# Sixteen stores of output rows asked for by GpSimd instead of SyncE

## The chip, the cores and the metric

The kernel runs on one core of one Trainium2 chip. A core has five engines that run beside each other: TensorE (PE; its weight loads are listed as PEld), VectorE (DVE), ScalarE (ACT), GpSimd (POOL) and SyncE (SP). Each works off its own queue in order. Transfers between the memories are asked for ("issued") by an engine's queue and carried out by 16 DMA engines that all queues share; a semaphore tells when a transfer has landed. The metric is the device time in microseconds (us); smaller is better.

## The reference, cut to what matters

A state-space convolution and a linear attention over the same length are mixed by a gate:

```python
x = A_u                                              # 1 x 2048 x 512
g = sigmoid((x * gate_w).sum(-1, keepdims=True))
# A: K = Re(sum_n C * exp(dt*A*l) * dt*B), y = irfft(rfft(u) * rfft(K))[:L] + u * Dskip
a = A_ref(x, A_re, A_im, B_re, B_im, C_re, C_im, log_dt, Dskip)
# B: 32 heads of 16: phi = [softmax(q w), softmax(-q w)]; o = phi_q (phi_k^T v) / (phi_q . sum phi_k); o @ wo
b = B_ref(B_x, wqkv, w_phi, wo)
return g * a + (1 - g) * b
```

The kernel writes one output, `out`, 2048 rows of 512 bf16 values, 2 MB.

## The kernel before, in words

All steps are nodes of one plan (`class Plan`). A node names an engine, a function that emits its instructions, and the nodes it depends on. The order in which the nodes are emitted is written out as a string of two-digit numbers (`ORDER`, line 74) and replayed by `Plan.run` (line 149); on each engine the instructions run in that order, each as soon as its semaphores allow. For nodes that can stand on either of two engines, a second string (`SIDES`) says which; `P.cur.at` is the engine of the node at hand. A transfer (`P.dma`, line 128) is a node on SP, or on SP or ACT where `eng=("SP", "ACT")` is given. Between queues nothing but semaphores orders the work.

The 512 channels are four quarters Q = 0 to 3 of 128. For each quarter the convolution kernel is generated in units of 32 channels (`kgen`, lines 1098 to 1120), brought to the frequency domain, multiplied with the input's spectrum that waits in DRAM (`XUX`), and brought back (`transform`, line 1190). For a "far" transform the half-done result `Zr` is written to DRAM (`Zd`, lines 1277 and 1279) and read back in another order (`ZT`, line 1289); both are issued by SP. The last product of a transform goes to PSUM (`psy`, line 1345 for a far one, line 1358 for the other kind), and VectorE multiplies it with the gate into the tile `xT` (lines 1367, 1370 and 1373), which by then holds the output. The last quarter is done in three transforms: units 12 and 13 together (64 channels, far), unit 14 (32 channels, far), and unit 15 (32 channels, not far).

The attention runs in four blocks of 512 rows (`block`). The first three add to the same PSUM tiles as the convolution. The last, block 3, is late: its result `bps` is brought to `xT` by ScalarE and VectorE (line 980 among others) for three quarters of the columns, all at once.

`xT` holds row 64 q + 4 j + c of the output in partition 32 c + q, at index j. A store therefore takes one c (32 partitions), a range of j, and a range of columns. There are two places that store, each of them a function `st(h)` that issues two stores, for c = 2h and 2h + 1:

- line 992, from node `outL` (line 995): the rows of block 3 (four j), 384 columns; four stores of 96 KB.
- line 1384, from node `out` (line 1398): after the transform of Q = 1 the columns of quarters 0 and 1 (12 j, 256 columns, four stores of 192 KB); after Q = 2 its 128 columns (12 j, four of 96 KB); after units 12 and 13 their 64 columns (16 j, four of 64 KB); and after unit 15 the last 64 columns (16 j, four of 64 KB). This last set is the one with `last` true. `SIDES` puts one of its two nodes on ACT; all other nodes of both places are on SP.

In `ORDER` the stores stand in this order: Q = 2, then Q = 0 and 1, then half of units 12 and 13, half of block 3, the other halves of both, and the last set. SP's queue has the write of the last `Zd` after the first four stores and the read of the last `ZT` after the next four.

GpSimd does the index ramps, masks and some fills at the start; it issues no transfer.

Of the kernel before, what the change touches and what calls it, by code (L numbers as in the profile page):

```python
# [10 lines left out]
ACT = mybir.ActivationFunctionType  # L11
# [798 lines left out]
def plan_queries(P, nc, g, psum, r):  # L810

    fc, act, at, xT = g.fc, g.act, g.at, g.xT
# [12 lines left out]
    def block(b, late, yn=()):  # L825
        Q, L = Bag(), "L" if late else ""
        eq = []
        a = None
        nm = 2 if late else 1
        for m0 in range(0, 4, nm):  # L830
# [19 lines left out]
            a = P.add("PE", "pq" + L, pq, [sh, sp] + g.Wqn + r["xt"] + ([a] if a else []), take=([psq] if late else ["bk"]) + ([] if m0 else ["r8"]))  # L850
# [64 lines left out]
        pb, po, ot, out = None, None, [], []  # L915
# [47 lines left out]
        for ip in range(2 if late else 0):  # L963
            j = 4 * b + 2 * ip
# [24 lines left out]
        if late:  # L989
            def st(h):  # L990
                for c in (2 * h, 2 * h + 1):
                    (nc.scalar if P.cur.at == "ACT" else nc.sync).dma_start(out=g.out2d[:, 0:384].rearrange("(q j c) d -> c q j d", q=32, j=16, c=4)[c][:, 4 * b:4 * b + 4],
                                      in_=xT[32 * c:32 * c + 32, 4 * b:4 * b + 4, 0:3, :].rearrange("p j a d -> p j (a d)"))
            for h in range(2):
                P.dma("outL", 1.2, 2.0, lambda h=h: st(h), on, move=0.8, cnt=2, eng=("SP", "ACT"))
# [61 lines left out]
def plan_conv(P, nc, g, psum, r):  # L1057

    fc, act, at, xT = g.fc, g.act, g.at, g.xT
# [130 lines left out]
    def transform(XA, ready, Q, off, nd, far, Ls, last, co=0, free=True, split=False):  # L1190
# [5 lines left out]
        pair = 1 if Q == 1 else 0  # L1196
        lo = 64 if last else off
        ov = g.out2d[:, 128 * (Q - pair) + lo:128 * Q + off + nd].rearrange("(q j c) d -> c q j d", q=32, j=16, c=4)
# [5 lines left out]
        for r0 in range(0, 32, ns):  # L1204
# [24 lines left out]
            def tt(k=None, r0=r0, box=box, end=end):  # L1229
# [11 lines left out]
                if k != 0:  # L1241
# [3 lines left out]
                    if not far:  # L1245
                        F.tt = box.t.rearrange("p k (r d) -> p k r d", d=nd)
                        box.t = None
            b = P.add("PE", "psB%d" % nd, sb, ready + [sk] + ([b] if r0 else []), take=[psq, "XK"] + (["r8"] if first else []),
                      drop=(["XA0"] if end and XA.drop else []))
# [68 lines left out]
        for j0 in range(0, 16, nj):  # L1318
# [62 lines left out]

            def st(h, js=slice(0, 12 if Q < 3 else 16)):
                for c in (2 * h, 2 * h + 1):
                    (nc.scalar if P.cur.at == "ACT" else nc.sync).dma_start(out=ov[c][:, js], in_=xT[32 * c:32 * c + 32, js, Q - pair:Q + 1, lo:off + nd].rearrange("p j a d -> p j (a d)"))
            ya = []
            if Q < 3:
                ya = [P.add("PE", "pya", pya, [sq] + [n for b in range(j0 // 4, min(3, j0 // 4 + 2)) for n in g.ot[b]] + ([y] if j0 else []), take=[psq], rw=("diagD", ""))]
# [8 lines left out]
            if end and Q != 0 and (nd > 32 or last):  # L1396
                for h in range(2):
                    P.dma("out", 1.2, 2.0, lambda h=h, st=st: st(h), on, move=(1.6 if pair else 1.05 if far and nd == 128 else 0.9), cnt=2, eng=("SP", "ACT"))
                on.clear()
# [18 lines left out]
    for k, (units, far) in enumerate(g.LAST):  # L1418
# [6 lines left out]
        off = 32 * (units[0] - 12)  # L1425
# [205 lines left out]
```

## Time and profile before

| | before |
|---|---|
| median of three runs | 260.86 us (260.01 to 261.76) |
| profiled execution, its own time | 259.96 us |
| its span, first to last instruction | 258.2 us |
| PE, DVE, ACT, POOL busy | 197.2, 227.3, 224.4, 11.2 us |
| stores of the output | 20: 18 issued by SP, 2 by ACT |

The profile's page gives busy times, a strip of 40 slices of 6.5 us, the chain of work that ended last and the costliest groups. A row of the timeline has the start in us from the start of the span, the length in us, the engine (a "q" behind it: its queue, that is, an issue), the line of the code, the operation, what it writes and reads, and how many instructions are merged. The listing of transfers gives the size of each and the median time from issue to landing. A row of the waits has who waited, for whom, the sum in us, how often, and the longest. A row of the windows has a stretch of time and how long each engine was busy in it.

### The profile page before, as it was taken

What the parts mean: (1) busy time and instruction counts of PE and PEld (TensorE: products, weight loads), DVE (VectorE), ACT (ScalarE), POOL (GpSimd) and SP (SyncE); (2) the same over time, 40 slices, a digit from 0 to 9 for tenths busy, and PEclk for the clock granted to TensorE, in tenths of its full rate; (3) what the DMA queues carried; (4) which work ended last, traced back from release to release, by engine and by line L of the source; (5) the groups of instructions that cost most, each with busy time, mean ns of one, the idle gap of its engine ahead of it and who ended that gap; (6) DMA issues with size and microseconds to landing.
All of it is one profiled execution on the core that took longest, in us unless ns stands there. A gap on an engine that the chain in (4) does not pass through costs nothing.

```text
span 258.2 us, 10095 instructions
## 1 busy us (share of the span) xinstructions
PE 197.2 (76%) x4512; PEld 132.2 (51%) x4512; DVE 227.3 (88%) x308; ACT 224.4 (87%) x312; POOL 11.2 (4%) x21
## 2 busy tenths in 40 slices
PE   0577899999962888789576858688977679989750
PEld 0466665665642542356345535474764556765530
DVE  6888799797899998999999999999999999978710
ACT  6999979998999999999999999999997989756210
POOL 5650000000000000000000000000000000000000
PEclk9999999999996587999979998999999999999985
DMA  6899100083710669105451449525768789776875
GB/s 200 142 206 208 45 3 1 5 250 70 226 30 0 201 198 280 63 4 161 130 135 34 120 110 244 164 46 162 193 157 212 196 217 252 208 219 120 200 101 98
DMA packets 67259, 36.19 MB, mean 140 GB/s; under 512 B 46352, under 2 KB 62864, under 8 KB 66832
## 3 DMA queue, kind: packets, MB, share of 16 engines
q1 hardware_dynamic: 66160, 35.42, 55.0%
q8 instruction: 35, 0.57, 0.9%
q10 hardware_dynamic: 1056, 0.13, 0.3%
q14 instruction: 8, 0.07, 0.1%
HBM read 22.17 MB, written 13.37 MB: 138 GB/s over the span
## 4 chain that ended last, share of the span: by engine, by line
ACT 43%; PE 35%; issue 7%; SPq 7%; DVE 4%; DMA 2%; ACTq 0%
ACT cs L68 9%; PE pk L705 6%; ACT Eq L68 5%; PE vp L753 4%; SPq L1497 4%; ACT XA L145 4%; ACT E L68 4%; PE psz L1263 3%; ACT L65 3%; ACT XK L145 3%; ACT Zr L145 3%; ACT xst L145 3%; PE psy L820 3%; PE kps L179 2%; ACT trg L68 2%
## 5 line engine op out<-in xcount | busy, mean ns | idle before, releaser
L1098 DVE TENSOR_TENSOR A<-Ctab,Dtab 128x2048 bf16<-128x2048 bf16 x32 | 38.7, 1222 | 0.8 <-PE kps L179 0.8
L68 ACT ACTIVATE cs<-args 128x1024 bf16<-128x1024 f32 x32 | 31.2, 1068 | 0.0
L179 PE MATMUL kps<-R,A 128*32 128x64 bf16 x1536 | 17.3, 199 | 7.9 <-DVE R L1120 1.9
L179 PEld LDWEIGHTS <-A 128*32 128x32 bf16 x1536 | 15.4, 116 | 11.9 <-DVE R L1120 4.0
L1120 DVE TENSOR_TENSOR R<-E,cs 128x2048 bf16<-128x2048 bf16 x16 | 19.5, 1222 | 0.0
L1116 DVE TENSOR_TENSOR R<-E,cs 128x2048 bf16<-128x2048 bf16 x16 | 19.4, 1222 | 0.0
L1263 PE MATMUL psz<-t,TI 128*128 128x512 bf16 x60 | 15.7, 387 | 3.4 <-ACT cs L68 1.5
L145 ACT CAST XK<-psB 128x1024 bf16<-128x1024 f32 (+1 forms) x17 | 16.8, 1016 | 0.4 <-PE psB L192 0.4
L145 ACT CAST Zr<-psz 128x1024 bf16<-128x1024 f32 x15 | 15.5, 1036 | 1.8 <-PE psz L1263 1.1
L1231 DVE TENSOR_TENSOR t<-XUX,XK 128x2048 bf16<-128x2048 bf16 x14 | 17.1, 1222 | 0.0
L68 ACT ACTIVATE E<-args 128x1024 bf16<-128x1024 f32 x16 | 17.1, 1066 | 0.0
L753 PE MATMUL vp<-WW,xT 128*128 128x512 bf16 x64 | 17.0, 398 | 0.0
L839 PE MATMUL pq<-xT,Wqp 128*128 128x512 bf16 x64 | 16.7, 405 | 0.3 <-ACT E L68 0.3
L68 ACT ACTIVATE Ek<-pk 128x512 bf16<-128x512 f32 x32 | 16.7, 600 | 0.2
L68 ACT ACTIVATE Eq<-pq 128x512 bf16<-128x512 f32 (+1 forms) x28 | 16.8, 695 | 0.2 <-PE pq L839 0.2
L612 PE MATMUL psB<-XAu,TB 64*128 64x128 bf16 x256 | 11.7, 256 | 6.2 <-ACT XAu L145 4.1
L145 ACT CAST XA<-psA 128x1024 bf16<-128x1024 f32 x15 | 15.1, 1046 | 0.2 <-PE psA L186 0.2
L705 PE MATMUL pk<-WW,xT 128*128 128x512 bf16 x64 | 15.2, 380 | 0.0
L612 PEld LDWEIGHTS <-TB 64*128 64x128 bf16 x256 | 10.0, 114 | 9.5 <-issue 9.0
L762 DVE TENSOR_TENSOR vr<-vb,vr 128x1024 bf16<-128x1024 bf16 x16 | 10.6, 688 | 3.0 <-ACT vr L68 2.7
L147 DVE CAST XAu<-psA 128x1024 bf16<-128x1024 f32 x9 | 10.6, 1218 | 2.7 <-PE psA L587 2.7
L65 ACT ACT_TABLE_LOAD x10 | 12.8, 1283 | 0.2
(206 smaller groups left out, 495.0 us busy)
## 6 DMA issues: line engine op xcount, KB each, us to landing
XUX<-XUd SPq DMA_DIRECT2D x32, 256.0 KB, 4.2
XUd<-xst SPq DMA_DIRECT2D x8, 512.0 KB, 3.3
ax<-apd SPq DMA_DIRECT2D x16, 256.0 KB, 4.8
Zd<-Zr SPq DMA_DIRECT2D x15, 256.0 KB, 4.1
ZT<-Zd SPq DMA_DIRECT2D x12, 256.0 KB, 4.8
UD<-in_A_u_dram SPq DMA_DIRECT2D x16, 128.0 KB, 4.4
XUd<-xst SPq DMA_DIRECT2D x8, 256.0 KB, 4.0
wqk<-in_B_wqkv_dram SPq DMA_DIRECT2D x1, 1024.0 KB, 5.7
```

What stands on the lines that cost most here:

```text
L65: return self.nc.scalar.preload_act_table_set(name)
L68: return self.nc.scalar.activation(**kw)
L145: self.nc.scalar.copy(out=o, in_=i)
L179: nc.tensor.matmul(kps[32 * dj:32 * dj + 32, g4, e, :], lhsT=A[:, d // 4, 32 * ka:32 * ka + 32, d % 4], rhs=R[:, kr, d, :], start=(i == 0) ...
L612: nc.tensor.matmul(box.ps[:, c2, sl, :], lhsT=fc.TB[rows, b0:b0 + 2].rearrange("p a b -> p (a b)"), rhs=X.t[rows, k, r0 + sl].rearrange("p ...
L705: nc.tensor.matmul(box.ps[:], lhsT=xT[:, st, kt, :], rhs=g.WW[:, kt, :], start=(kt == 0), stop=(kt == 3))
L753: nc.tensor.matmul(box.ps[:], lhsT=xT[:, st, kt, :], rhs=g.WW[:, 4 + kt, :], start=(kt == 0), stop=(kt == 3))
L1098: nc.vector.tensor_tensor(out=c.A[:, :, 64 * k:64 * k + 64, :].rearrange("p q (x b) l -> p x b q l", b=8), in0=cf.unsqueeze(2).to_broadcas ...
L1116: nc.vector.tensor_tensor(out=c.R[:, :, :, 32:64], in0=t.E[:, 1].unsqueeze(1).to_broadcast([128, 2, 32, 32]), in1=t.cs[:], op=ALU.mult)
L1120: nc.vector.tensor_tensor(out=c.R[:, :, :, 0:32], in0=t.E[:, 0].unsqueeze(1).to_broadcast([128, 2, 32, 32]), in1=t.cs[:, ::-1, :, ::-1], o ...
L1231: nc.vector.tensor_tensor(out=box.t, in0=Ls[r0 // ns].X[:], in1=box.XK[:].unsqueeze(1).to_broadcast([128, 2, 1024]), op=ALU.mult)
L1263: nc.tensor.matmul(box.ps[:, hb, :], lhsT=fc.TIp[:, k].rearrange("p h a t -> p (h a t)"), rhs=box.t[:, k, 512 * hb:512 * hb + 512], start= ...
```

## The change

At both places the issuing engine becomes GpSimd. At line 1384 the last set is left out of this: it stays on ACT for one half and on SP for the other. So 16 of 20 stores move: four of 192 KB, eight of 96 KB and four of 64 KB. What is stored, from where and to where is unchanged, and so are `ORDER` and `SIDES`: the nodes are emitted at the same places, only onto another queue.

```diff
         if late:
             def st(h):
                 for c in (2 * h, 2 * h + 1):
-                    (nc.scalar if P.cur.at == "ACT" else nc.sync).dma_start(out=g.out2d[:, 0:384].rearrange("(q j c) d -> c q j d", q=32, j=16, c=4)[c][:, 4 * b:4 * b + 4],
+                    nc.gpsimd.dma_start(out=g.out2d[:, 0:384].rearrange("(q j c) d -> c q j d", q=32, j=16, c=4)[c][:, 4 * b:4 * b + 4],
                                       in_=xT[32 * c:32 * c + 32, 4 * b:4 * b + 4, 0:3, :].rearrange("p j a d -> p j (a d)"))
...
             def st(h, js=slice(0, 12 if Q < 3 else 16)):
                 for c in (2 * h, 2 * h + 1):
-                    (nc.scalar if P.cur.at == "ACT" else nc.sync).dma_start(out=ov[c][:, js], in_=xT[32 * c:32 * c + 32, js, Q - pair:Q + 1, lo:off + nd].rearrange("p j a d -> p j (a d)"))
+                    (nc.scalar if P.cur.at == "ACT" else nc.sync if last else nc.gpsimd).dma_start(out=ov[c][:, js], in_=xT[32 * c:32 * c + 32, js, Q - pair:Q + 1, lo:off + nd].rearrange("p j a d -> p j (a d)"))
```

## Prediction, written before the result was known

> **What bounds the kernel now.** I read the page first, then the chain of waits, then the last 21 us queue by queue, because nothing is stored to the output before that.
>
> ```profile
> span 258.2 us, 10095 instructions
> ...
> POOL 5650000000000000000000000000000000000000
> ```
>
> The last GpSimd work ends near 16 us; its queue is empty afterwards. The listing of DMA issues gives the stores:
>
> ```profile
> out_dram<-xT SPq DMA_DIRECT2D x8, 96.0 KB, 2.8
> out_dram<-xT SPq DMA_DIRECT2D x4, 192.0 KB, 4.7
> ...
> out_dram<-xT SPq DMA_DIRECT2D x6, 64.0 KB, 2.3
> ...
> out_dram<-xT ACTq DMA_DIRECT2D x2, 64.0 KB, 2.8
> ```
>
> That is 20 stores: 18 on SP, two on ACT. The last set is four of 64 KB, two on SP and two on ACT; the other 16 move. In order of time (start, length, engine, line), SP's queue and then what the stores wait for:
>
> ```profile
> 236.95 3.00 SPq L1384 DMA_DIRECT2D out_dram<-xT  x4
> 240.06 0.43 SPq L1279 DMA_DIRECT2D Zd<-Zr  x1
> 240.53 3.18 SPq L1384 DMA_DIRECT2D out_dram<-xT  x4
> 243.83 3.54 SPq L1289 DMA_DIRECT2D ZT<-Zd  x4
> 247.48 2.20 SPq L1384 DMA_DIRECT2D out_dram<-xT  x2
> 249.78 1.05 SPq L992 DMA_DIRECT2D out_dram<-xT  x2
> 250.87 2.12 SPq L1384 DMA_DIRECT2D out_dram<-xT  x2
> 253.04 1.29 SPq L992 DMA_DIRECT2D out_dram<-xT  x2
> 254.43 1.27 SPq L1384 DMA_DIRECT2D out_dram<-xT  x2
> ```
>
> ```profile
> 235.71 1.22 DVE L1370 TENSOR_TENSOR xT<-psy,gT 128x1024 bf16<-128x1024 f32 x1
> ...
> 242.52 1.22 DVE L1370 TENSOR_TENSOR xT<-psy,gT 128x1024 bf16<-128x1024 f32 x1
> 243.66 1.13 DVE L980 TENSOR_SCALAR xT<-bps,gT 128x384 bf16<-128x384 f32 x2
> ...
> 251.44 0.69 DVE L1370 TENSOR_TENSOR xT<-psy,gT 128x512 bf16<-128x512 f32 x1 [0.74 <-PE psy L1345]
> ```
>
> ```profile
> 237.11 1.01 ACT L145 CAST Zr<-psz 128x1024 bf16<-128x1024 f32 x1
> ...
> 252.21 1.37 ACTq L1384 DMA_DIRECT2D out_dram<-xT  x2
> ```
>
> SP is backed up. The last arithmetic ends at 251.44 + 0.69 = 252.13. ACT asks for its half of the last set at once, at 252.21. SP's half has the same data but stands behind eight other stores and goes out at 254.43, 2.3 us later. The windows around these issues give issue-to-landing times, first for ACT's second store, then for the pair of 96 KB, then for SP's last pair:
>
> ```profile
> out_dram<-xT ACTq DMA_DIRECT2D x1, 64.0 KB, 3.1
> ```
>
> ```profile
> out_dram<-xT SPq DMA_DIRECT2D x2, 96.0 KB, 2.6
> ```
>
> ```profile
> out_dram<-xT SPq DMA_DIRECT2D x2, 64.0 KB, 2.2
> ```
>
> SP's last store starts half way through the pair, at 254.43 + 0.64 = 255.07, and lands at 255.07 + 2.2 = 257.27. The closing steps take 258.2 - 257.27 = 0.93. So SP's queue sets the end, not an engine. The profiled execution took 259.96 us, 1.76 more than its span, and 0.9 below the median of the runs, 260.86; I apply the sum to both.
>
> **What leaves SP.** 16 issues: 3.00 + 3.18 + 2.20 + 1.05 + 2.12 + 1.29 = 12.8 us of SP's queue. Two things stood behind them. First, SP's half of the last set: it can go at 252.2, and its second store at 252.2 + 0.64 = 252.8. ACT's second store starts at about 252.21 + 0.69 = 252.9 and lands 3.1 later, at 256.0. The other landing row, 2.2, would make it 255.1; I take 3.1, because GpSimd's stores will be in flight beside it. Second, the small round trip over DRAM of the last far set: Zr is done at 237.11 + 1.01 = 238.12, but its write goes out only at 240.06, behind four stores, 1.9 us late, and the read back ZT stands behind four more. With SP free, ZT lands about 2 us sooner. What that is worth is read from who waits for it:
>
> ```profile
> PEld L1345 <- DMA ZT<-Zd: 0.4, 1, 0.4
> ...
> PE psz L1301 <- issue: 1.3, 1, 1.3
> PE psy L1358 <- issue: 1.2, 1, 1.2
> ```
>
> TensorE waited 0.4 us for ZT before the last product; ahead of it, it is held by the other product L1358 and by gaps that no releaser explains ("issue", 1.3 and 1.2 us), which I leave as they are. So 0.4 us of the 2 us comes out: the last arithmetic ends at 251.7. SP's and ACT's end becomes 256.0 - 0.4 = 255.6, and with 0.93 the span 256.5.
>
> **What is added.** GpSimd gets 16 issues in a row. They keep their order, so the four whose data are ready at 235.71 + 1.22 = 236.93 come first, and the four of 192 KB, which SP asks for at 240.53 without a wait for data, stand behind them. The rest is ready at 242.52 + 1.22 = 243.74 and 243.66 + 1.13 = 244.79, before GpSimd gets there if an issue takes over (243.74 - 236.93) / 8 = 0.85 us. Nothing else is queued behind these waits on GpSimd, and no engine waits for a store; only the end does. With p us for one issue, the last one is out at 236.93 + 16p and lands 2.6 later (the 96 KB row, the size of the last one); this reaches 255.6 at p = 1.0, today's 257.27 at p = 1.11, and 2.6 us more, one per cent of the time, at p = 1.27. Each 0.1 us of p is 1.6 us of time. This price decides the case, and the trace has no DMA issued by GpSimd. The nearest rows, from SP's issues of the same stores and from GpSimd's own instructions:
>
> ```profile
> L1384 SPq DMA_DIRECT2D out_dram<-xT x14: 321/602/1594, 237.0 to 255.1; - x14
> ```
>
> ```profile
> 10.41 2.34 POOL L454 TENSOR_TENSOR selE<-m,b 128x1024 bf16<-128x1024 bf16 x1
> ...
> 13.85 0.86 POOL L487 MEMSET SSw<- 128x264 bf16 x1
> ...
> 15.25 0.12 POOL L491 MEMSET eps<- 128x1 f32 x1
> ```
>
> From below: 0.32, SP's shortest, which hides everything behind the readiness of the data; GpSimd's own instruction overhead, 0.12, is lower still. From above: 2.34, its dearest instruction, which ends at 236.93 + 37.4 + 2.6 + 0.93 = 277.9. I take 1.0: above SP's median 0.60 and just above the 0.86 of a GpSimd instruction that writes a few hundred elements, since a store is not one run of bytes: by its access pattern it is 32 partitions by 4, 12 or 16 rows, thus 128, 384 or 512 pieces, and somebody has to list them. The last store then lands at 236.93 + 16.0 + 2.6 = 255.5, level with the last set's 255.6.
>
> The Trainium skill speaks against the change here: "DMA: Bandwidth & Descriptors", section "SWDGE vs HWDGE vs iDMA", says that DMAs from GpSimd have their descriptors written by a program on its cores, and "Latency and other measured facts" gives about 1 us to the first byte, against 0.6 from SP. No run so far shows it; by that extra 0.4 us GpSimd's last store would land at 255.9 and the gain would be 1.4 instead of 1.7 us.
>
> The sum: 258.2 - 256.5 = 1.7 us off. Own time 259.96 - 1.7 = 258.3; against the median 260.86 - 1.7 = 259.2. A measurement of this kernel (runs from 260.01 to 261.76) can tell about one per cent, 2.6 us, from no change, so this counts as within it.
>
> **Rivals.**
>
> *GpSimd becomes the bound (slower).* Its place is the row of 16 issues from 236.93, its price p, and it decides from p = 1.11. For it: GpSimd is slow per element (0.86 us for 264 elements of a memset), and 12 of the 16 stores have 384 or 512 pieces. Against: SP needs 0.60. At p = 1.5 the last store lands at 236.93 + 24 + 2.6 = 263.5, the span is 264.5, and the time 260.86 + 6.3 = 267.1.
>
> *VectorE locks GpSimd out (slower).* If GpSimd cannot list pieces while VectorE works, VectorE's busy time is added to its row:
>
> ```profile
> core 0: us, PE busy (x) PEld busy (x) DVE busy (x) ACT busy (x) POOL busy (x), PEclk, DMA share, GB/s
> 236.90:245.00 8.10, 6.86 (x250) 4.96 (x249) 5.84 (x10) 2.66 (x5) 0.00 (x0) 1.00 0.78 171
> 245.00:252.10 7.10, 3.28 (x203) 2.36 (x203) 1.51 (x3) 1.07 (x2) 0.00 (x0) 0.82 0.75 106
> ...
> 236.90:258.20 21.30, 10.15 (x453) 7.32 (x452) 7.39 (x13) 3.73 (x7) 0.00 (x0) 0.80 0.71 129
> ```
>
> VectorE (DVE) is busy for 7.39 us. GpSimd ends at 236.93 + 16 + 7.4 = 260.3, the last store lands at 262.9, span 263.9: 260.86 + 5.7 = 266.5. Against it: most of VectorE's operations there read psy, psA or bps at full f32 size and not two bf16 tiles. The rule stands in the Trainium skill, "SBUF — State Buffer", in the box on the "DVE blocks DMA" trap, which names VectorE's two-port modes, and says elsewhere that tensor_tensor has none; no run here has shown it.
>
> *The transfers bound the end (no effect).* In the last of these rows the 16 DMA engines are busy 0.71 of the time (the share ahead of the GB/s). If GpSimd's stores are still queued on them when the last set goes out, its landing stretches, as the 192 KB stores' 4.7 does; then 252.9 + 4.7 + 0.93 = 258.5, and the time is 260.86 + 0.3 = 261.2. About the same time results where p lies a little over 1.11.
>
> *More comes out.* If the last set lands in 2.2 instead of 3.1 and GpSimd is done by then, the span is 256.5 - 0.9 = 255.6; a gap of 1.2 on TensorE that shrinks with quieter queues would add to that. The time is 259.2 - 0.9 = 258.3, or down to 257.1 with such a gap gone.
>
> That the stores would stay on SP is excluded by the diff: lines 992 and 1384 name the engine.
>
> **How the numbers follow.** Forecast 0.42, at 259.2, its own range 258.3 (the last set lands in 2.2) to 260.7 (p = 1.1). GpSimd as the bound by over one per cent 0.28; VectorE's lock 0.04; no effect 0.16; more comes out 0.10. Faster by over one per cent: the last case and a little of the forecast, 0.13. Slower by over one per cent: the first two, 0.32. The rest, 0.55, within. The range is 257.6 to 267.1: below, the middle of the case in which more comes out; above, p = 1.5, with about 0.1 left out at either end.
>
> **What would show it.** Right: SP's pair of L1384 starts within 0.2 us of ACT's; Zd is written by 238.5; 16 issues on GpSimd's queue from 236.9, about 1 us apart, the last out by 253; the closing line waits for a store of the last set, or for both. Wrong: GpSimd's issues run past 254.7 and the closing line waits for one of line 992; gaps in GpSimd's row that match VectorE's operations; or landings of the last set over 4 us.

## The result and the profile after

The changed kernel takes 259.94 us (median of 20 runs, 258.45 to 261.74) against 261.45 us before (20 runs beside it, 259.99 to 263.25): ratio 0.9942, 95% interval 0.9918 to 0.9965. That is 1.5 us off, where 1.7 was forecast, and under the one per cent that was called telling. The profiled execution of the changed kernel took 260.65 us with a span of 258.9, so it is one of the longer ones of its 20.

From the page of the changed kernel: the strip of GpSimd and the queues (packets, MB, share of the DMA engines), among them a new one, q0:

```profile
span 258.9 us, 10101 instructions
...
POOL 5540000000000000000000000000000000000770
...
DMA packets 62139, 36.19 MB, mean 140 GB/s; under 512 B 42768, under 2 KB 57296, under 8 KB 61712
...
q0 software_dynamic: 768, 1.84, 3.1%
```

The listing of its transfers (issues, KB each, us from issue to landing):

```profile
out_dram<-xT POOLq DMA_DIRECT2D x8, 96.0 KB, 3.4
out_dram<-xT POOLq DMA_DIRECT2D x4, 192.0 KB, 5.5
...
ZT<-Zd SPq DMA_DIRECT2D x4, 64.0 KB, 5.4
out_dram<-xT POOLq DMA_DIRECT2D x4, 64.0 KB, 4.0
...
out_dram<-xT ACTq DMA_DIRECT2D x2, 64.0 KB, 2.6
out_dram<-xT SPq DMA_DIRECT2D x2, 64.0 KB, 2.2
```

Its timeline, for SP, GpSimd, ACT's queue and the operations of VectorE that the stores wait for:

```profile
239.65 0.34 SPq L1279 DMA_DIRECT2D Zd<-Zr  x1
243.29 5.67 SPq L1289 DMA_DIRECT2D ZT<-Zd  x4
254.55 1.33 SPq L1384 DMA_DIRECT2D out_dram<-xT  x2
...
239.12 5.12 POOL L1384 DMA_DIRECT2D out_dram<-xT  x8 [223.41 <-ACT xT L145]
245.85 1.27 POOL L1384 DMA_DIRECT2D out_dram<-xT  x2 [1.61 <-issue]
247.11 1.12 POOL L992 DMA_DIRECT2D out_dram<-xT  x2
248.22 1.30 POOL L1384 DMA_DIRECT2D out_dram<-xT  x2
249.48 1.13 POOL L992 DMA_DIRECT2D out_dram<-xT  x2
...
254.54 1.62 ACTq L1384 DMA_DIRECT2D out_dram<-xT  x2
...
237.22 1.22 DVE L1370 TENSOR_TENSOR xT<-psy,gT 128x1024 bf16<-128x1024 f32 x1
...
253.77 0.69 DVE L1370 TENSOR_TENSOR xT<-psy,gT 128x512 bf16<-128x512 f32 x1 [0.74 <-PE psy L1345]
```

The span is not shorter here, since this execution came to its first store 1.5 us later (237.22 against 235.71). Two stretches can be compared instead. The *arithmetic* of the end runs from the start of the L1370 row at 235.71 (237.22) to the end of the last one; the *rest* from there to the end of the span. Before: 252.13 - 235.71 = 16.42, and 258.2 - 252.13 = 6.07. After: 254.46 - 237.22 = 17.24, and 258.9 - 254.46 = 4.44. SP's and ACT's halves of the last set now leave together, at 254.55 and 254.54, 0.1 us after the last arithmetic. So the rest shrank by 1.6 us, and the arithmetic grew by 0.8.

### The profile page after: what moved, and what is told of

It reads as the page before. It is cut to its first block, busy times and chain, and to the rows that moved or that the text cites. A ratio compares the mean times of both kernels' runs of the same rounds, so it can differ in the third digit from the quotient of the medians.

```text
span 258.9 us, 10101 instructions
## 1 busy us (share of the span) xinstructions
PE 195.5 (76%) x4512; PEld 133.2 (51%) x4512; DVE 228.8 (88%) x308; ACT 224.5 (87%) x312; POOL 20.0 (8%) x37
## 2 busy tenths in 40 slices
DMA packets 62139, 36.19 MB, mean 140 GB/s; under 512 B 42768, under 2 KB 57296, under 8 KB 61712
## 3 DMA queue, kind: packets, MB, share of 16 engines
q1 hardware_dynamic: 60272, 33.58, 52.4%
q0 software_dynamic: 768, 1.84, 3.1%
## 5 line engine op out<-in xcount | busy, mean ns | idle before, releaser
L1384 POOL DMA_DIRECT2D out_dram<-xT x12 | 7.7, 649 | 225.0 <-ACT xT L145 223.4
L1263 PE MATMUL psz<-t,TI 128*128 128x512 bf16 x60 | 16.2, 396 | 3.0 <-ACT cs L68 1.6
L839 PE MATMUL pq<-xT,Wqp 128*128 128x512 bf16 x64 | 15.4, 380 | 0.3 <-ACT E L68 0.3
L186 PE MATMUL psA<-W,KD 128*64 128x128 bf16 x256 | 10.0, 223 | 4.3 <-ACT XK L145 1.7
```

Source lines behind the costliest of these rows:

```text
L839: nc.tensor.matmul(box.ps[:, m - m0, :] if late else box.ps[:], lhsT=g.Wqp[:, kt, 128 * m:128 * m + 128], rhs=xT[:, 4 * b:4 * b + 4, kt, : ...
L1263: nc.tensor.matmul(box.ps[:, hb, :], lhsT=fc.TIp[:, k].rearrange("p h a t -> p (h a t)"), rhs=box.t[:, k, 512 * hb:512 * hb + 512], start= ...
```

## The experiments

The ratios are against the kernel before, run beside each; the two stretches come from the one profiled execution of each run. The kernels with the early eight left out do not write those rows of the output. The edits are cut to the lines that change. "Program loads" is the name in the expectations for what may fill TensorE's gaps without a releaser ("issue" in the rows of waits): the profile lists an instruction queue (q8, 35 packets, 0.57 MB), but no run shows that loading is what makes these gaps.

| run | ratio (95% interval) | arithmetic | rest |
|---|---|---|---|
| before; before again, twice | 1 | 16.42; 16.26, 15.88 | 6.07; 6.56, 6.08 |
| the change; again, twice | 0.9942 (0.9918 to 0.9965) | 17.24; 16.99, 16.44 | 4.44; 4.45, 4.44 |
| last set's half alone on GpSimd | 0.9992 (0.9959 to 1.0025) | 15.93 | 6.32 |
| early eight alone | 1.0029 (1.0000 to 1.0057) | 16.22 | 6.16 |
| late eight alone | 0.9953 (0.9922 to 0.9985) | 15.86 | 4.42 |
| the change, 192 KB stores first | 1.0003 (0.9967 to 1.0039) | 16.96 | 4.37 |
| the change, early eight left out | 0.9896 (0.9852 to 0.9941) | 15.87 | 4.41 |
| before, early eight left out | 0.9970 (0.9940 to 1.0000) | 15.35 | 6.45 |
| the change, stores in halves | 1.0063 (1.0029 to 1.0098) | 15.44 | 8.48 |
| late eight alone, 192 KB behind ZT | 1.0023 (0.9994 to 1.0052) | 15.60 | 6.59 |

### Only SP's half of the last set on GpSimd

```diff
-  (nc.scalar if P.cur.at == "ACT" else nc.sync).dma_start(out=ov[c]...
+  (nc.scalar if P.cur.at == "ACT" else nc.gpsimd if last else nc.sync).dma_start(out=ov[c]...
```

> Everything as before, but SP's half of the last set is issued by GpSimd, the other 16 stores stay on SP. Theory (SP's backlog ahead of the last set is what the change removes): GpSimd's two stores start within 0.2 us of ACT's pair, some 2 us sooner than SP's did; but SP's last 96 KB store, issued 1.8 us after the last arithmetic and landing 2.6 later, now ends the span, so only part of the gain comes: 0.8 us, ratio 0.997 (0.994 to 1.000). Rival (the early return of ZT and an empty SP queue are the gain): no gain, ratio 1.000 or above.

No gain that can be told from none, at the upper edge of what the theory allowed. Its timeline at the end, SP, GpSimd and ACT:

```profile
252.06 1.17 SPq L992 DMA_DIRECT2D out_dram<-xT  x2
251.69 1.50 POOL L1384 DMA_DIRECT2D out_dram<-xT  x2 [236.57 <-DVE xT L1370]
251.06 1.37 ACTq L1384 DMA_DIRECT2D out_dram<-xT  x2
```

GpSimd starts 251.69 - 250.98 = 0.7 us after the last arithmetic, not within 0.2 of ACT as I expected, and SP is still asking for block 3 until 253.23. The position of the last pair alone is therefore not what counts: whatever stands behind the backlog ends late.

### The early eight alone, and the late eight alone

```diff
-  ... else nc.sync).dma_start(out=ov[c]...
+  ... else nc.gpsimd if Q < 3 else nc.sync).dma_start(out=ov[c]...
```

> Only the eight early stores (quarters 0 to 2, four of 96 KB and four of 192 KB) go to GpSimd; the other ten of SP stay there. Theory: SP's last pair again stands behind eight stores and ZT, so the last set leaves no more than 0.3 us sooner after the last arithmetic than before, and the eight stores beside ZT and beside TensorE's program loads stretch the arithmetic by 0.8 us (16.4 to 17.2 us from the first store's data to the last arithmetic): no gain, ratio 1.000 (0.997 to 1.003). Rival (Zd and ZT leaving 2 us sooner is the gain): at least half of the gain of the change, ratio 0.997 or below.

```diff
-  ... else nc.sync).dma_start(out=g.out2d[:, 0:384]...
+  nc.gpsimd.dma_start(out=g.out2d[:, 0:384]...
-  ... else nc.sync).dma_start(out=ov[c]...
+  ... else nc.sync if last or Q < 3 else nc.gpsimd).dma_start(out=ov[c]...
```

> Only the eight late stores (units 12 and 13, and block 3) go to GpSimd; the eight early ones stay on SP ahead of Zd and ZT. Theory: the last set leaves at once, 2.3 us sooner; Zd and ZT leave as late as before; no large stores of GpSimd run beside ZT, so the arithmetic stays at 16.4 us: 2.0 to 2.4 us off, ratio 0.992, better than the whole change's 0.9942 by 0.5 us. Rival (ZT's early leaving matters): worse than the whole change, 1.0 us off, ratio 0.996.

The end of SP's queue and ACT's with the early eight on GpSimd:

```profile
250.38 1.68 SPq L992 DMA_DIRECT2D out_dram<-xT  x2
252.16 2.22 SPq L1384 DMA_DIRECT2D out_dram<-xT  x2
...
251.11 1.39 ACTq L1384 DMA_DIRECT2D out_dram<-xT  x2
```

and with the late eight on GpSimd, SP and ACT:

```profile
241.99 3.60 SPq L1289 DMA_DIRECT2D ZT<-Zd  x4
250.34 1.33 SPq L1384 DMA_DIRECT2D out_dram<-xT  x2
...
250.35 1.60 ACTq L1384 DMA_DIRECT2D out_dram<-xT  x2
```

With the early eight moved no time is gained, as the theory had it, but not for its reasons. The arithmetic did not stretch (16.22), and SP's half leaves 252.16 - 251.04 = 1.1 us after the last arithmetic, where before it was 2.3: half of the delay is gone, where the theory had allowed 0.3 us. The rest is 6.16 all the same. Part of it is that the pair takes 2.22 us instead of 1.27; SP's waits have a row for this, ahead of the second store:

```profile
SPq L1384 <- DMA out_dram<-xT: 1.0, 1, 1.0
```

With the late eight moved, SP has nothing between ZT and the last set, the rest is 4.42 and the ratio 0.9953, which cannot be told from the whole change's 0.9942. So the late eight carry all of the gain that was measured; the early eight on GpSimd add none that can be measured. That the late eight alone would be better than the change by 0.5 us was not borne out: 0.9953 is nearer to the rival's 0.996 than to 0.992.

### The 192 KB stores ahead of the 96 KB ones

```diff
+        for n in [n for n in self.nodes if n.name == "out"][:2]:
+            order.remove(n.i)
+            order.insert(1 + max(order.index(d.i) for d in n.deps), n.i)
```

> The whole change, and the four 192 KB stores are emitted as soon as their data are there, some 10 us ahead of the 96 KB ones instead of behind them. Theory (the stores of GpSimd beside ZT and the program loads cost the arithmetic 0.8 us): the 192 KB stores are gone before Zd, ZT lands some 2 us sooner, the arithmetic takes 16.4 us or less: 2.3 to 3 us off, ratio 0.990. Rival (the DMA engines are busy anyway and the place of the stores does not matter): as the change, ratio 0.994.

Both expectations missed: the gain is gone, 1.0003. The profiled execution is the longest of its twelve (265.42 us), so its size is no measure, but its rows show what those stores met. First the listing in a window around SP's two XUX loads, then the timeline:

```profile
XUX<-XUd SPq DMA_DIRECT2D x2, 256.0 KB, 7.9
```

```profile
228.15 2.67 POOL L1384 DMA_DIRECT2D out_dram<-xT  x4 [212.92 <-ACT KD L142]
...
231.52 3.67 SPq L1185 DMA_DIRECT2D XUX<-XUd  x2
...
241.06 1.29 DVE L1234 TENSOR_TENSOR t<-XUX,XK 128x1024 bf16<-128x1024 bf16 x2 [4.48 <-ACT xT L142]
```

The two loads that follow the four stores took 7.9 us to land (3.7 for the same two in the changed kernel), and VectorE's product with them began after 4.48 us of idling. The profile names ACT as its releaser, by a row that ends just then (240.66 + 0.39 = 241.05) but writes xT, which the product does not read. The second of the two loads, asked for at 233.7, landed 7.3 us later, at 241.0. So the likely cause is the load. The rest is 4.37 as in the change: what was lost lies ahead of the last set. Whether it is so in the shorter executions too was not seen.

### The early eight left out, with and without GpSimd

```diff
-  for c in (2 * h, 2 * h + 1):
+  for c in (2 * h, 2 * h + 1) if Q == 3 else ():
```

> The whole change, with the eight early stores (quarters 0 to 2) left out of the work: those output rows are not written. Theory (beside freeing SP ahead of the last set, the change puts GpSimd's large stores beside ZT and TensorE's program loads, which took the arithmetic from 16.4 to 17.25 us): arithmetic 16.0 us or less, time from last arithmetic to the end 4.4 us as in the whole change, ratio 0.990. Rival (the arithmetic varies by itself from execution to execution, whatever is in flight): arithmetic 16.2 to 17.3, ratio 0.994.

> The kernel before, with the same eight early stores left out: no store on GpSimd at all. Theory (only SP's backlog counts): SP asks for ZT some 2 us sooner and is through with the eight late stores before the last arithmetic, so the last set leaves at once; 4.4 us from the last arithmetic to the end, ratio 0.990 as without them in the changed kernel. Rival (it takes GpSimd's queue, as the issues of SP stretch with ZT): 5.5 us or more from the last arithmetic to the end, ratio 0.996.

Without these stores the changed kernel comes to 0.9896, some 0.5% lower, from only four executions, and the intervals of the two overlap. The arithmetic is 15.87, as the theory had it, but the kernel before, with all its stores, came to 15.88 in one of its repetitions. Without the early eight and without GpSimd, SP and ACT end thus:

```profile
251.58 1.10 SPq L992 DMA_DIRECT2D out_dram<-xT  x2
253.28 3.91 SPq L1384 DMA_DIRECT2D out_dram<-xT  x2
253.33 1.62 ACTq L1384 DMA_DIRECT2D out_dram<-xT  x2
```

The theory was right that SP is through in time: its half leaves at 253.28, with ACT's. But SP's second store is late; the pair takes 3.91 us where it takes 1.33 in the changed kernel, and the rest stays at 6.45. SP's waits say what the 2.6 us are:

```profile
SPq L1384 <- DMA out_dram<-xT: 2.7, 1, 2.7
```

The second store was held until an earlier transfer to the output had landed, the same wait as with the early eight on GpSimd, and longer. With the late eight on GpSimd no such row appears. So an SP queue that has caught up was not enough in this execution, and the reason the rival gave (issues that stretch beside ZT) is not the one seen: the four ZT issues took 2.78 us. Why the last store has to wait for an earlier one, and whether it does so in every execution, is open. The ratio, 0.997, is next to the rival's 0.996.

### GpSimd's stores in halves

```diff
+  for s in (4 * b, 4 * b + 2): nc.gpsimd.dma_start(...[:, s:s + 2], in_=xT[..., s:s + 2, 0:3, :]...)
+  for js in ... (slice(0, 6), slice(6, 12)) if Q < 3 else (slice(0, 8), slice(8, 16)): ...
```

> The whole change, each of GpSimd's 16 stores cut in two halves by rows: 32 issues, the same pieces and bytes. Theory (an issue of GpSimd costs 0.62 us whatever its pieces, and GpSimd has about 3 us to spare): 32 x 0.6 = 19.5 us plus about 2 us of waits for its earlier stores, so it asks for the last one near 258.5 and the end is 4 to 5 us later than before; ratio 1.015 to 1.020. Rival (the price goes by pieces or bytes): no more than the whole change, ratio 0.994.

Its timeline, and from the listing by line the lengths (ns, least, median, most) of an issue, of the changed kernel and of this one:

```profile
237.91 11.46 POOL L1384 DMA_DIRECT2D out_dram<-xT  x20 [221.81 <-ACT xT L145]
249.40 2.12 POOL L992 DMA_DIRECT2D out_dram<-xT  x4
251.52 2.31 POOL L1384 DMA_DIRECT2D out_dram<-xT  x4
253.82 2.12 POOL L992 DMA_DIRECT2D out_dram<-xT  x4
...
251.50 1.62 ACTq L1384 DMA_DIRECT2D out_dram<-xT  x2
```

```profile
L1384 POOL DMA_DIRECT2D out_dram<-xT x12: 617/622/847, 239.1 to 248.9; - x12
...
L992 POOL DMA_DIRECT2D out_dram<-xT x4: 560/571/592, 247.1 to 250.0; - x4
```

```profile
L1384 POOL DMA_DIRECT2D out_dram<-xT x24: 565/567/794, 237.9 to 253.2; - x24
```

Half the pieces cost 567 ns instead of 622: an issue of GpSimd has a price of its own of about half a microsecond, and the pieces add little. 32 issues end at 253.82 + 2.12 = 255.94, 4.5 us after the last arithmetic (251.42); GpSimd's stores now end the kernel, and it is slower than before, 1.0063. The direction is as expected; the size is not (1.015 to 1.020), because I had added 2 us of waits that are not there and counted 0.6 instead of 0.57.

### The 192 KB stores on SP behind the read of ZT

To the run of the late eight alone, a reordering of SP's queue:

```diff
+        z = [n for n in self.nodes if n.name == "zr"][-1].i
+        o = [n.i for n in [n for n in self.nodes if n.name in ("out", "out_d", "out_w")][:6]]
+        order = [k for i in order if i not in o for k in [i] + (o if i == z else [])]
```

> Only the eight late stores on GpSimd, as in the run of the late eight alone (0.9953), and SP's four 192 KB stores emitted behind the read of ZT instead of ahead of it. Theory (the 192 KB stores ahead of ZT cost the arithmetic the 0.4 us that TensorE waited for ZT, and some of the program loads' time): arithmetic 15.5 us, 4.4 us from it to the end, ratio 0.992. Rival (ZT is early enough, the program loads set the arithmetic): ratio 0.995.

In the plan each of the two store nodes of these columns has two bookkeeping nodes beside it, hence the six that are moved. The arithmetic is 15.60 as the theory had it, yet the ratio is 1.0023. The listing in the window of the last set:

```profile
out_dram<-xT SPq DMA_DIRECT2D x2, 64.0 KB, 4.6
out_dram<-xT ACTq DMA_DIRECT2D x2, 64.0 KB, 4.8
```

The last set leaves on time but lands in 4.6 and 4.8 us instead of 2.2 and 2.6, behind 768 KB that was asked for just ahead of it, and the rest is 6.59. None of these versions beats the change clearly.

### Both kernels again

> The changed kernel unaltered, once more under the profiler, to see what of its stage lengths stays. Theory (the arithmetic of the last stage varies by itself from execution to execution; what the change moves is the time behind it): arithmetic anywhere from 15.4 to 17.3 us, 4.4 us from its end to the end of the span. Rival (GpSimd's stores stretch the arithmetic in every execution of this kernel): arithmetic 16.9 us or more again.

> The kernel before, unaltered, once more under the profiler. Theory: arithmetic from 15.4 to 17.3 us, 6.0 to 6.4 us from its end to the end of the span. Rival: arithmetic 16.4 us or less.

> As the first repetition of the changed kernel: theory 15.4 to 17.3 and 4.4 us; rival 16.9 us or more.

> As the first repetition of the kernel before: theory 15.4 to 17.3 and 6.0 to 6.4 us; rival 16.4 us or less.

The last rows of VectorE, in the first repetition of the change and of before:

```profile
237.96 1.22 DVE L1370 TENSOR_TENSOR xT<-psy,gT 128x1024 bf16<-128x1024 f32 x1
...
254.26 0.69 DVE L1370 TENSOR_TENSOR xT<-psy,gT 128x512 bf16<-128x512 f32 x1 [0.74 <-PE psy L1345]
```

```profile
237.78 1.22 DVE L1370 TENSOR_TENSOR xT<-psy,gT 128x1024 bf16<-128x1024 f32 x1
...
253.35 0.69 DVE L1370 TENSOR_TENSOR xT<-psy,gT 128x512 bf16<-128x512 f32 x1 [0.74 <-PE psy L1345]
```

The rest is 4.44, 4.45 and 4.44 with the change, 6.07, 6.56 and 6.08 before: 1.8 us less in the mean, every time. The arithmetic averages 16.9 with the change and 16.2 before; the lowest of the one (16.44) is just above the highest of the other (16.42). The theory's range for the arithmetic held and the rival's (16.9 or more each time with the change) did not; of the rests, 6.56 lies outside the 6.0 to 6.4 that was expected. With three against three a lengthening by some 0.7 us is likely rather than excluded. Together -1.8 + 0.7 = -1.1 us, inside the timed interval of -0.9 to -2.1.

## Why the prediction came out right

*SP's queue sets the end: right.* The forecast had SP's last pair leave with ACT's, within 0.2 us, and the whole time from the last arithmetic to the end go from 6.07 to 3.9 + 0.93 = 4.8 us. It went to 4.44 or 4.45 in all three profiles. The part that was mis-sized is the landing: I took 3.1 us; in the changed kernel it is 2.6 on ACT and 2.2 on SP. The late eight alone reproduce this. The early eight alone do not, nor does a GpSimd issue of the last pair alone.

*The price of an issue: mis-sized, on the harmless side.* I took p = 1.0; it is 0.62 for 384 or 512 pieces and 0.57 for 128. With that the eight early issues take 5.12 us, less than the 6.81 to the data of the ninth, so GpSimd waits for data, as the bound at 0.85 said. It is out of stores at 249.48 + 1.13 = 250.61, 3.9 us before the last arithmetic ends. The rival in which GpSimd becomes the bound did not come, and the halves show that it is near: twice the issues, and the kernel is slower than before.

*Zd and ZT leave sooner, the arithmetic ends 0.4 us sooner: wrong.* They do leave sooner: from the start of the arithmetic ZT's read is asked for after 243.29 - 237.22 = 6.07 us, before after 8.12. But the four issues then take 5.67 us instead of 3.54 and land in 5.4 instead of 3.8, so the last is out after 11.74 against 11.66. What the earlier start gave, the longer issues and landings took back. I had taken the reads to keep their length and not asked which stores they would lie beside. The 0.4 us itself rested on a row that I read wrongly. The wait for ZT belongs to an earlier transform; the timeline of the kernel before has it at 227.76, and at the last product none:

```profile
227.76 0.45 PEld L1345 LDWEIGHTS <-TJ 64*32 64x32 bf16 x32 [0.42 <-DMA ZT<-Zd]
...
250.67 0.59 PEld L1345 LDWEIGHTS <-TJ 64*32 64x32 bf16 x64 [0.41 <-issue]
```

No profile here names a wait for ZT before the last product, so nothing showed that 0.4 us could come out there. Nor did the arithmetic get shorter: TensorE's gaps without a releaser, which I left as they were, make up most of the difference.

```profile
PE psz L1301 <- issue: 1.9, 1, 1.9
...
PE psy L1358 <- issue: 1.3, 1, 1.3
```

In the changed kernel they are 1.9 and 1.3, before 1.3 and 1.2: 0.7 of the 0.8 us. In the repetitions their sums are 3.1 and 2.5 with the change and 2.8 and 2.0 without it, so they vary about as much from execution to execution. What makes them long is open. That GpSimd's early stores beside them do it is in line with the changed kernel without these stores (15.87) and the late eight alone (15.86), and spoken against by the early eight alone (16.22) and by the halves (15.44), which have the same bytes in flight.

*VectorE's lock: no sign of it.* The eight early issues of GpSimd take 5.12 us in one row without a gap, while VectorE is busy for 3.8 of them; issues of the same line take 617 ns at least and 622 in the median. The one gap in GpSimd's row, 1.61 us, ends 0.6 us after the data of the ninth store, as its first issue starts 0.7 us after its data. The trap that the Trainium skill describes ("SBUF — State Buffer", the box on "DVE blocks DMA") does not show with the operations that run here. The Trainium skill's figures for the first byte ("DMA: Bandwidth & Descriptors", "Latency and other measured facts") point the right way for the stores of 96 KB, which land 3.3 to 3.5 us after GpSimd's issue, against 2.7 to 2.8 after SP's, in three profiles each. Those of 192 KB took 5.5, 4.7 and 4.7 against 4.7, 4.8 and 4.3, which shows no clear difference.

*Transfers as the bound: not in the change,* where the last set lands no later after its issue than before (2.6 and 2.2 us against 2.8 and 2.2); but late landings are what was seen with the 192 KB stores behind ZT.

That the sum came so close is partly luck, for two errors offset each other in part: by the means of three profiles the rest gained 0.5 us more than forecast, and the arithmetic lost 0.7 where 0.4 was to be gained. That makes 1.1 us off instead of 1.7; the timed 1.5 lies between, and the stretches of single profiles vary by as much as these differences.

## What to carry to other kernels

Look at who stands in the queue ahead of the last transfer: a store issued from the same data 2.3 us later than its twin on another engine is time that can be won by moving its predecessors; moving the pair itself won nothing here. It is enough to move those that lie just ahead of it: moving the earlier ones let the small reads start sooner, but these then took longer. Whether ScalarE, which in the kernel before has no work from 247.4 us to the last set at 252.2, would carry the late eight as well as GpSimd was not tried. Count the issues of GpSimd, not their pieces, and check that the row ends before the last data are there.

## What the runs showed of the hardware that was not expected

- An issue on GpSimd took 0.53 to 0.67 us for 64 to 512 pieces (0.79 to 0.85 for the first of a row), about the same as SP's median of 0.60 for the same stores. The first of a row began 0.7 us after its data (251.69 against 250.98 with the last set's half on GpSimd), ACT's 0.1 us.
- GpSimd's stores went in fewer and larger packets: 768 for 1.84 MB, where SP's queue had used 5888 for the same bytes (66160 before, 60272 after); 62139 in all instead of 67259.
- SP's ZT issues were slow where whole early stores of GpSimd were in flight (4.94 to 5.67 us for four, in four profiles) and not where the same bytes came in halves (3.07) or from SP (3.19 to 4.04 in five profiles); the listing of the halves has

```profile
ZT<-Zd SPq DMA_DIRECT2D x4, 64.0 KB, 3.2
```

against 5.4. The cause was not tried.
- With the early eight on GpSimd or left out and the late eight on SP, SP's last store waited 1.0 and 2.7 us for an earlier store to land; in the other runs no store of SP has such a row.
